# F in 64x64 tiles with its blocks ordered by the copies, and the masks of the first two groups back on VectorE

## The chip, the cores and the metric

The kernel runs on one core of a Trainium2 chip. The metric is the device time of one execution in microseconds; of the kernel before there are three: 876.13, 878.44 and 879.28 us, median 878.44. The profile is that of one execution whose span was 874.4 us. All data is 32-bit floating point at the inputs, except the two weight matrices of the feed forward, which the kernel converts from 64-bit on the chip.

The engines are called by their names or by the profile's short forms: TensorE (PE for matmuls, PEld for the loads of its weights), VectorE (DVE), ScalarE (ACT), GpSimd (POOL) and SyncE (SP, which here only issues transfers). PSUM is the memory that TensorE writes into.

## The reference

Two blocks follow each other: a recurrent attention with a state per batch and head, and a feed forward with a hard swish.

```python
batch, n_heads, seq, head_dim = (4, 8, 768, 40)
for t in range(S):
    y[:, :, t] = np.einsum('bhd,bhde->bhe', rt, state)
    Sa = np.einsum('bhde,bhe->bhd', state, at)
    state_decay = state * wt[:, :, None, :] - np.einsum('bhd,bhe->bhde', Sa, bt)
    state = state_decay + np.einsum('bhd,bhe->bhde', vt, kt)
# ... bridge: (B,H,S,D) -> (B*S, H*D) = (3072, 320)
h = x @ w_in                       # 320 -> 2048
relu6 = np.clip(h + 3.0, 0.0, 6.0)
g = h * relu6 / 6.0
return (g @ w_out)                 # 2048 -> 320
```

The kernel does not step through the 768 times one by one. It takes blocks of 64 times, and within a block it solves a triangular system: with the decays divided out, the products of all a with all earlier b in a block form a strictly triangular 64x64 matrix F per head, and the inverse of (1 - F) gives all `Sa` of the block at once. Products of k with a (called E), of v with r (C) and of u with r (H) are wanted for earlier times only, so these 64x64 scores are masked to a strict triangle.

## The kernel before

There are 24 units: 12 blocks of time by two pairs of batches; the two batches of a pair lie in the two halves of the partitions. Four units are a group; F of a group is kept for 4 x 8 = 32 heads, and its inverse is made on VectorE by substitution over 32 columns of the diagonal 32x32 blocks (`invert`, 60 small products and sums with waits between), after which TensorE adds the off-diagonal block (`third_block`). So F's 64x64 matrix of a head is used in two pieces: its two diagonal 32x32 blocks, which the inversion reads at columns 0 to 31 of F's tile, and the lower off-diagonal block, which `third_block` reads at columns 32 to 63 of the lower 32 rows.

The kernel has three phases. In the first, the four units of the first group are prepared by twos, the first inversion runs on VectorE, and the weights are converted by VectorE and ScalarE in small steps between. In the second, the four units of the first group take their scan steps in staggered chains, while the weights are finished and the second group is prepared. In the third, the stages of four units at a time and the feed forward of finished units share TensorE to the end. All engines take their instructions in the order in which the program emits them.

F of a unit, in tiles of 32 columns of at; each 32x64 result lands in its own quarter of the partitions, and for the lower rows (c = 1) the two 32-column halves of bt are read in reverse order, so that the diagonal block always lands at columns 0 to 31:

```python
        def f_stage():

            f = ps_pair(NPR, BL)
            for pr in range(NPR):
                for c in range(2):
                    for q in range(2):
                        for s in range(2):
                            x = q * BL + c * L
                            y = o["bt"][half(s, D), pr, half(q)].rearrange("p (c t) -> p c t", c=2)
                            if c:
                                y = y[:, ::-1, :]
                            z = (q ^ s) * BL + c * L
                            nc.tensor.matmul(out=f[s][z:z + L, pr, :],
                                             lhsT=o["at"][half(s, D), pr, x:x + L], rhs=y,
                                             start=True, stop=True, tile_position=(s * SLOT, z))
            yield PE
            for s in range(2):
                x = n * H + 4 * s
                nc.scalar.activation(out=F[:, x:x + 4, :], in_=f[s], func=AF.Copy, scale=-1.0)
```

The masks. In the first two groups (`early`) ScalarE copies the scores out of PSUM and GpSimd sets the unwanted triangle to zero; later VectorE copies only the wanted elements into a tile whose other elements stay zero:

```python
    def masked(o, early):

        turn[0] += 1
        x = score[turn[0] % len(score)]
        if early:
            for i in range(2):
                nc.scalar.activation(out=x[:, 4 * i:4 * i + 4, :], in_=o[i], func=AF.Copy)
            for q in range(2):
                nc.gpsimd.affine_select(
                    out=x[half(q)], in_=x[half(q)], pattern=[[0, H], [1, BL]],
                    compare_op=ALU.is_gt, fill=0.0, base=0, channel_multiplier=-1)
            return x
        for i in range(2):
            nc.vector.copy_predicated(out=x[:, 4 * i:4 * i + 4, :], mask=mask4, data=o[i])
        return x
# ...
            o["E"] = masked(x, i < 2 * NU)      # e_stage, NU = 4
# ...
            m["K"] = masked(x, i < NU)          # s_C
# ...
            m["B"] = masked(x, i < NU)          # s_H
```

The first stage of a step, with the fetch of the next unit's r (four transfers of 40 KB) on ScalarE's queue for units 1 to 3:

```python
        def s_RT():
            x = turn_pairs(o["RN"])
            yield PE
            m["RT"] = turned("RT")
            nc.scalar.activation(out=m["RT"][:], in_=x[:], func=AF.Copy)
            fetch("R", i + 1, nc.scalar if i < NU - 1 else nc.sync)
            scale = tmp.tile([P, 2, NPR], F32, name="scale", bufs=2)
            nc.gpsimd.tensor_tensor(out=scale[:], in0=last_dec[p][:], in1=dec[:, 0], op=ALU.mult)
            nc.gpsimd.tensor_copy(last_dec[p][:], dec[:, 1])
            nc.vector.tensor_tensor(out=st[:, :, :, 0:D], in0=st[:, :, :, 0:D],
                                    in1=_ap(scale[:], 0, [[NPR, 2], [1, NPR], [0, D]]), op=ALU.mult)
```

The conversion of a weight piece takes 5 steps; a step is a turn of this generator, and there are 40 pieces:

```python
                nc.vector.tensor_scalar(x, hi, 20, 0x7FF, ALU.logical_shift_right,
                                        ALU.bitwise_and)
                nc.scalar.activation(out=x, in_=x, func=AF.Relu, bias=low[:], scale=2.0 ** 23)
                yield
# ... (m likewise, then two scalar_tensor_tensor on VectorE)
                nc.vector.tensor_tensor(out=dst, in0=mf, in1=xf, op=ALU.mult)
                converted[0] += 1
                load()
                yield
```

The second phase, with the weight steps that go beside the stages:

```python
    for t in range(LAST + OWN):
        for i in range(NU):
            if 0 <= t - APART * i < OWN and t - APART * i != 11:
                if t - APART * i < 2:
                    block(i, t - APART * i)
                run(chains[i], weight=3 if t else 12)
        # ... the second group's loads and preparation
        elif t >= OWN + 1:
            pieces(1)                           # feed forward of finished units
```

Of the kernel before, what the change touches and what calls it, by code (L numbers as in the profile page):

```python
# [11 lines left out]
ALU = mybir.AluOpType  # L12
AF = mybir.ActivationFunctionType
# [3 lines left out]
P = 128  # L17
BL = 64
HB = BL // 2
L = 32  # L20
# [9 lines left out]
def kernel(  # L30
# [42 lines left out]
    nc = tc.nc  # L73
    B, H, T, D = r.shape
    NG = T // (2 * BL)
    NPR = H // 2
    NP = B // 2
    NU = 2 * NP
# [29 lines left out]
    def ps_pair(*dims):  # L108

        n = 1  # L110
        for d in dims:
            n *= d
        if shared[0] is None or shared[1] + n > 512:
            shared[:] = [ps_any([P, 512]) for _ in range(2)], 0
        at = shared[1]
        shared[1] += n
        views, step = [], n
        for d in dims:
            step //= d
            views.append([step, d])  # L120
        return [_ap(t[:], at, views) for t in shared[0]]
# [6 lines left out]
        out=ident[:], in_=ones, pattern=[[1, P]],  # L128
        compare_op=ALU.is_equal, fill=0.0, base=0, channel_multiplier=-1,
# [3 lines left out]
        out=ones[:, 0:BL], in_=ones[:, 0:BL], pattern=[[1, BL]],  # L133
# [185 lines left out]
    PE, DONE = 1, 2  # L319
# [4 lines left out]
    def fetch(name, i, engine=None):  # L324

        if i is None or i >= NK:
            return
        x, crossed = {"W": (w, 0), "A": (a, 0), "B": (b, 0), "K": (k, 0), "R": (r, 1),
                      "V": (v, 1)}[name]
        if name == "V":  # L330
            t = values[i % AHEAD]
        else:
            t = (others if i < 2 * NU and i % 2 and name != "R" else inputs)[name]
        g, p = names[i]
        engine = engine or nc.sync
# [30 lines left out]
    def half(i, n=SLOT):  # L366
        return slice(SLOT * i, SLOT * i + n)
# [10 lines left out]
                                     rhs=rhs[half(i, D), n, half(q)], start=True, stop=True)  # L378
        return o

    def masked(o, early):

        turn[0] += 1
        x = score[turn[0] % len(score)]
        if early:
            for i in range(2):
                nc.scalar.activation(out=x[:, 4 * i:4 * i + 4, :], in_=o[i], func=AF.Copy)
            for q in range(2):
                nc.gpsimd.affine_select(  # L389
                    out=x[half(q)], in_=x[half(q)], pattern=[[0, H], [1, BL]],  # L390
                    compare_op=ALU.is_gt, fill=0.0, base=0, channel_multiplier=-1)
            return x
        for i in range(2):
            nc.vector.copy_predicated(out=x[:, 4 * i:4 * i + 4, :], mask=mask4, data=o[i])  # L394
        return x


    def prepare(i, F):
# [45 lines left out]
            bt = o["bt"] = turned("bt")  # L444
            nc.vector.tensor_tensor(out=bt[:], in0=x[:], in1=o["rg"][:], op=ALU.mult)

        def f_stage():

            f = ps_pair(NPR, BL)
            for pr in range(NPR):  # L450
# [12 lines that stand above are left out]
            for s in range(2):  # L463
                x = n * H + 4 * s
                nc.scalar.activation(out=F[:, x:x + 4, :], in_=f[s], func=AF.Copy, scale=-1.0)

        def factor_stage():

# [28 lines left out]
        def e_stage():  # L497
            x = scores(o["kt"], o["at"])
            yield PE
            o["E"] = masked(x, i < 2 * NU)  # L500

        def ev_stage():

# [9 lines left out]
            for q in range(2):  # L513
# [1 line left out]
                    nc.scalar.activation(out=EV[half(q ^ s), s], in_=ev[q][half(q ^ s)], func=AF.Copy)  # L515
            o["EV"] = EV

        return {"W": w_stage, "gam": gam_stage, "A": a_stage, "B": b_stage, "F": f_stage,
                "factor": factor_stage, "K": k_stage, "E": e_stage, "EV": ev_stage}

    def in_turn(stages, order):
# [81 lines left out]
    def step(i):  # L603
# [6 lines left out]
        def s_RT():  # L610
            x = turn_pairs(o["RN"])
            yield PE
            m["RT"] = turned("RT")
            nc.scalar.activation(out=m["RT"][:], in_=x[:], func=AF.Copy)  # L614
            fetch("R", i + 1, nc.scalar if i < NU - 1 else nc.sync)
            scale = tmp.tile([P, 2, NPR], F32, name="scale", bufs=2)
            nc.gpsimd.tensor_tensor(out=scale[:], in0=last_dec[p][:], in1=dec[:, 0], op=ALU.mult)
            nc.gpsimd.tensor_copy(last_dec[p][:], dec[:, 1])
            nc.vector.tensor_tensor(out=st[:, :, :, 0:D], in0=st[:, :, :, 0:D],
                                    in1=_ap(scale[:], 0, [[NPR, 2], [1, NPR], [0, D]]), op=ALU.mult)  # L620
# [49 lines left out]
        def s_C():  # L670
            x = scores(m["VT"], m["RT"])
            yield PE
            m["K"] = masked(x, i < NU)

        def s_UT():

# [50 lines left out]
        def s_H():  # L727
            x = scores(m["UT"], m["RT"], swap=True)
            yield PE
            m["B"] = masked(x, i < NU)  # L730

        def s_y():
            y = ps_pair(NPR, BL)
# [154 lines left out]
    def run(stage, steps=0, weight=0, mixed=0):  # L888

        for at in stage:  # L890
            if at == DONE:
                return
            aside(steps, mixed)
            for _ in range(weight):
                next(weights, None)
# [64 lines left out]
    for t in range(LAST + OWN):  # L960
        for i in range(NU):
            if 0 <= t - APART * i < OWN and t - APART * i != 11:
                if t - APART * i < 2:
                    block(i, t - APART * i)
                run(chains[i], weight=3 if t else 12)
        if t == LAST + 2:
            seconds()
            for name in "WA":
                fetch(name, NU + 1)
            third.clear()  # L970
            second_group = by_twos(NU, 3, 0, 1.25)
# [98 lines left out]
    m = 0  # L1070
# [59 lines left out]
```

## Time and profile before

| engine | busy us | share of the span |
|---|---|---|
| TensorE, matmuls | 787.2 | 90% |
| TensorE, weight loads | 670.8 | 77% |
| VectorE | 529.8 | 61% |
| ScalarE | 297.2 | 34% |
| GpSimd | 177.1 | 20% |

A busy time is the union of an engine's instructions, so matmuls that overlap in different tiles of the array are not counted twice. In the groups, one row stands for all instructions of a line and form: `L459 PE MATMUL any<-bt,at 40*32 40x64` are matmuls with 40 rows and 32 columns of weights on 64 moving columns, from tiles bt and at into a PSUM tile called any. The trace has two matmul records for each 32-bit matmul. After the bar come the busy time and the mean of one in ns, then the idle time of the engine just before these instructions, and what ended it. In a timeline each row is a run of equal instructions: start, time, engine, line, count, and in brackets the idle time before it with its releaser. The line numbers are those of the kernel before; L389 and L387 are the selections and copies of the early masks, L394 the predicated copies, L459 and L465 the matmuls and copies of F.

The costliest matmuls are those of the feed forward: L839 with 231.9 us, L815 with 195.3 and L820 with 55.8. The longest idle time that the chain of waits names at the end is 7.59 us after the last matmul.

### The profile page before, as it was taken

How to read it: one execution, taken by the hardware profiler on the slowest of the kernel's cores; microseconds unless marked ns; L12 is line 12 of the kernel's file. 1: busy time of each engine (PE TensorE's matmuls, PEld its weight loads, DVE VectorE, ACT ScalarE, POOL GpSimd, SP SyncE). 2: the span in 40 equal slices, each digit the busy share in tenths (PEclk: the TensorE clock that was granted, in tenths of full speed). 3: DMA queues.
4: the chain of work that ended last, by engine and by line, in shares of the span. 5: the costliest groups of instructions: out<-in, count | busy, mean ns of one | idle time of the engine just before them, and what ended most of it. 6: DMA issues, size and time to landing. Idle time of an engine off the chain costs nothing.

```text
span 874.4 us, 36298 instructions
## 1 busy us (share of the span) xinstructions
PE 787.2 (90%) x16128; PEld 670.8 (77%) x16128; DVE 529.8 (61%) x1109; ACT 297.2 (34%) x726; POOL 177.1 (20%) x327
## 2 busy tenths in 40 slices
PE   4710987888999999999999999999999999999998
PEld 4510865777888788887888888888888888888886
DVE  7899777677855669834579543787545774221211
ACT  1433754333334322442322433223433224232211
POOL 4441122243112230320220221211212102000000
PEclk9755559999999999999999999999999999999999
DMA  6543443242033331322321222121232101100000
GB/s 132 88 108 92 123 116 85 48 75 45 14 52 61 57 59 26 60 37 42 59 40 36 56 49 49 39 50 34 45 62 42 24 21 27 24 21 12 19 18 15
DMA packets 175979, 45.08 MB, mean 52 GB/s; under 512 B 157904, under 2 KB 173264, under 8 KB 175824
## 3 DMA queue, kind: packets, MB, share of 16 engines
q1 hardware_dynamic: 171504, 42.12, 24.3%
q8 instruction: 127, 2.08, 1.0%
q10 hardware_dynamic: 4320, 0.66, 0.5%
q14 instruction: 28, 0.23, 0.1%
HBM read 34.08 MB, written 3.93 MB: 43 GB/s over the span
## 4 chain that ended last, share of the span: by engine, by line
PE 69%; DVE 5%; issue 3%; DMA 1%; ACT 1%; POOL 1%; SPq 0%; POOLq 0%; DVEq 0%; ACTq 0%
PE o L839 22%; PE h L815 18%; PE h L820 5%; PE any L358 5%; PE any L376 3%; PE any L717 2%; PE any L740 2%; PE any L459 2%; PE any L628 1%; PE any L593 1%; PE any L662 1%; PE any L581 1%; DVE x L558 1%; DVE prod L552 1%; PE any L699 1%
## 5 line engine op out<-in xcount | busy, mean ns | idle before, releaser
L839 PE MATMUL o<-wout,gt 128*128 128x320 f32 x768 | 231.9, 447 | 1.1 <-issue 1.1
L815 PE MATMUL h<-xt,win 128*128 128x128 f32 x1536 | 195.3, 280 | 0.4 <-DVE gt L826 0.4
L815 PEld LDWEIGHTS h<-xt,win 128*128 128x128 f32 x1536 | 184.0, 193 | 10.4 <-DVE gt L826 0.9
L839 PEld LDWEIGHTS o<-wout,gt 128*128 128x128 f32 x768 | 140.1, 191 | 55.7 <-issue 2.2
L826 DVE SCALAR_TENSOR_TENSOR gt<-gt,h 128x512 f32<-128x512 f32 x96 | 61.4, 681 | 110.3 <-ACT gt L825 110.3
L825 ACT ACTIVATE gt<-h,three 128x512 f32<-128x512 f32 x96 | 60.8, 684 | 157.5 <-PE h L820 157.5
L750 POOL TENSOR_TENSOR yg<-ys,gam 128x512 f32<-128x512 f32 x24 | 41.1, 1715 | 193.9 <-DVE ys L747 130.8
L552 DVE TENSOR_TENSOR prod<-x 128x30 f32<-128x30 f32 (+9 forms) x180 | 63.7, 354 | 12.9 <-POOL x L543 8.2
L482 POOL TENSOR_TENSOR KBt<-K,rgt 128x320 f32<-128x320 f32 x24 | 24.5, 1022 | 221.5 <-ACT rgt L474 207.8
L558 DVE TENSOR_TENSOR x<-x,prod 128x30 f32<-128x30 f32 (+9 forms) x180 | 63.6, 353 | 4.4
L820 PE MATMUL h<-xt,win 64*128 64x128 f32 x768 | 55.8, 285 | 0.0
L820 PEld LDWEIGHTS h<-xt,win 64*128 64x128 f32 x768 | 46.6, 187 | 5.3 <-issue 0.2
L421 DVE RECIPROCAL gam<-prods 128x256 f32<-128x256 f32 x24 | 41.4, 1739 | 13.4 <-POOL yg L750 13.1
L747 DVE TENSOR_TENSOR ys<-any,ys 128x256 f32<-128x256 f32 x48 | 18.1, 419 | 49.8 <-PE any L509 29.7
L410 DVE TENSOR_TENSOR_SCAN prods<-wm,start 128x528 f32<-128x528 f32 x24 | 30.1, 1253 | 22.7 <-ACT wm L407 21.1
L724 DVE TENSOR_TENSOR state<-any,state 128x160 f32<-128x160 f32 x48 | 13.2, 316 | 49.1 <-PE any L376 49.1
L436 DVE RECIPROCAL rgam<-prods 128x256 f32<-128x256 f32 x24 | 41.7, 1737 | 0.0
L394 DVE COPY_PREDICATED score<-mask,any 128x256 f32<-128x256 int32 x112 | 41.3, 433 | 0.0
L581 PE MATMUL any<-tb,F 32*32 32x32 f32 x768 | 16.0, 199 | 24.9 <-DVE tb L561 24.8
L267 ACT ACTIVATE parts<-parts,low 128x256 uint32<-128x256 uint32 x40 | 20.3, 508 | 49.8 <-DVE parts L265 45.6
L740 PE MATMUL any<-score,KBt 64*64 64x64 f32 x1536 | 31.1, 227 | 6.2 <-POOL score L389 6.2
L614 ACT ACTIVATE RT<-any 128x512 f32<-128x512 f32 x24 | 14.3, 596 | 65.2 <-PE any L358 65.1
(138 smaller groups left out, 1205.8 us busy)
## 6 DMA issues: line engine op xcount, KB each, us to landing
raw<-in_moe_w_out_dram SPq DMA_DIRECT2D x20, 256.0 KB
B<-in_b_dram SPq DMA_DIRECT2D x48, 80.0 KB
K<-in_k_dram SPq DMA_DIRECT2D x48, 80.0 KB
V<-in_v_dram SPq DMA_DIRECT2D x96, 40.0 KB
out_dram<-ob SPq DMA_DIRECT2D x48, 80.0 KB
R<-in_r_dram SPq DMA_DIRECT2D x84, 40.0 KB
W<-in_w_dram SPq DMA_DIRECT2D x40, 80.0 KB
A<-in_a_dram SPq DMA_DIRECT2D x40, 80.0 KB
```

What stands on the lines that cost most here:

```text
L358: nc.tensor.transpose(out=o[:, n, :], in_=x[:, 2 * n:2 * n + 2, :].rearrange("p s e -> p (s e)"), identity=ident[:])
L394: nc.vector.copy_predicated(out=x[:, 4 * i:4 * i + 4, :], mask=mask4, data=o[i])
L421: nc.vector.reciprocal(gv[:, :, 0:HB], o["prods"][:, :, 0, 1:HB + 1][:, :, ::-1])
L436: nc.vector.reciprocal(rv[:, :, HB:BL], o["prods"][:, :, 1, 1:HB + 1])
L552: nc.vector.tensor_tensor(out=pv, in0=_ap(x[:], (i + 1) * L + i, [[L, n], [0, i]]), in1=_ap(x[:], i * L, [[0, n], [1, i]]), op=ALU.mult,)
L558: nc.vector.tensor_tensor(out=rest, in0=rest, in1=pv, op=ALU.add)
L740: nc.tensor.matmul(out=y[q][half(s), pr, :], lhsT=o[name][half(q), h * D:h * D + SLOT], rhs=m[name][half(q), 4 * rs + 2 * s + j, :], start ...
L815: nc.tensor.matmul(out=hp[c][:, i, :], lhsT=win[:, t, j * P:(j + 1) * P], rhs=xt[:, t, :], start=(t == 0 and i == 0), stop=False)
L820: nc.tensor.matmul(out=hp[c][:, i, :], lhsT=win2[half(c), (j0 + i) * P:(j0 + i + 1) * P], rhs=xt[half(c), 2, :], start=False, stop=(i == N ...
L825: nc.scalar.activation(out=gt[:], in_=hp[c][:], func=AF.Relu, bias=three[:], scale=1.0)
L826: nc.vector.scalar_tensor_tensor(out=gt[:], in0=gt[:], scalar=6.0, in1=hp[c][:], op0=ALU.min, op1=ALU.mult)
L839: nc.tensor.matmul(out=op[:], lhsT=gts[c][:, n, :], rhs=wout[:, c * HJ + r * NQ + n, :], start=((split or r == 0) and c == 0 and n == 0), ...
```

## The change

F is made in 64x64 tiles from the ninth unit on: a matmul takes 64 columns of at in place of 32, so there are half as many, and the reversal of the halves for the lower rows is done by the copies out of PSUM, which take each quarter of the partitions by itself. The upper 32 rows need only their first 32 columns. It is for TensorE, which is given fewer instructions for the same products. In place of this the kernel before has three other arrangements, which go: the early masks on ScalarE and GpSimd, which were to take work from VectorE, the r of units 1 to 3 on ScalarE's queue, and 12 weight steps in the first turn of the second phase.

```diff
-    def masked(o, early):
-
+    def masked(o):
         turn[0] += 1
         x = score[turn[0] % len(score)]
-        if early:
-            for i in range(2):
-                nc.scalar.activation(out=x[:, 4 * i:4 * i + 4, :], in_=o[i], func=AF.Copy)
-            for q in range(2):
-                nc.gpsimd.affine_select(
-                    out=x[half(q)], in_=x[half(q)], pattern=[[0, H], [1, BL]],
-                    compare_op=ALU.is_gt, fill=0.0, base=0, channel_multiplier=-1)
-            return x
         for i in range(2):
             nc.vector.copy_predicated(out=x[:, 4 * i:4 * i + 4, :], mask=mask4, data=o[i])
         return x
# ... f_stage is renamed f_by_32, and beside it stands
+        def f_by_64():
+
+            f = ps_pair(NPR, BL)
+            for pr in range(NPR):
+                for q in range(2):
+                    for s in range(2):
+                        nc.tensor.matmul(out=f[s][half(q ^ s), pr, :],
+                                         lhsT=o["at"][half(s, D), pr, half(q)],
+                                         rhs=o["bt"][half(s, D), pr, half(q)],
+                                         start=True, stop=True)
+            yield PE
+            for s in range(2):
+                x = n * H + 4 * s
+                for z in range(0, P, BL):
+                    nc.scalar.activation(out=F[z:z + L, x:x + 4, 0:L], in_=f[s][z:z + L, :, 0:L],
+                                         func=AF.Copy, scale=-1.0)
+                    y = f[s][z + L:z + BL].rearrange("p r (c t) -> p r c t", c=2)
+                    nc.scalar.activation(
+                        out=F[z + L:z + BL, x:x + 4, :].rearrange("p h (c t) -> p h c t", c=2),
+                        in_=y[:, :, ::-1, :], func=AF.Copy, scale=-1.0)
# ...
-            o["E"] = masked(x, i < 2 * NU)
+            o["E"] = masked(x)
# ... (s_C and s_H likewise)
-        return {"W": w_stage, "gam": gam_stage, "A": a_stage, "B": b_stage, "F": f_stage,
+        return {"W": w_stage, "gam": gam_stage, "A": a_stage, "B": b_stage, "F": f_by_32 if i < 2 * NU else f_by_64,
# ... in s_RT
-            fetch("R", i + 1, nc.scalar if i < NU - 1 else nc.sync)
+            fetch("R", i + 1)
# ... in the second phase
-                run(chains[i], weight=3 if t else 12)
+                run(chains[i], weight=3)
```

More of the change, by code (lines that the diff above doesn't have):

```diff
@@ L445, in b_stage, with f_by_32 @@
             nc.vector.tensor_tensor(out=bt[:], in0=x[:], in1=o["rg"][:], op=ALU.mult)
-        def f_stage():
+        def f_by_32():
             f = ps_pair(NPR, BL)
@@ L672, in s_C @@
             yield PE
-            m["K"] = masked(x, i < NU)
+            m["K"] = masked(x)
         def s_UT():
@@ L729, in s_H @@
             yield PE
-            m["B"] = masked(x, i < NU)
+            m["B"] = masked(x)
         def s_y():
```

## The prediction

> **What bounds the kernel now.** I read the page's table of slices first, because a mean hides stages with different limits.
>
> ```profile
> PE   4710987888999999999999999999999999999998
> DVE  7899777677855669834579543787545774221211
> PEclk9755559999999999999999999999999999999999
> ```
>
> A slice is 874.4 / 40 = 21.9 us. From slice 9 on (about 180 us) TensorE is busy 90% or more to the end: what is saved there counts only if it is TensorE time. Before that there are two other stages: slices 2 and 3, in which TensorE is nearly idle and VectorE full (the first inversion and the conversion of the weights), and slices 4 to 8, in which TensorE works at half clock or waits (the first four scan steps). The table by stretches gives the sizes (columns: stretch, its length, busy us and count of PE, PEld, DVE, ACT, POOL, then clock, DMA share, GB/s):
>
> ```profile
> 60.00:80.00 20.00, 0.00 (x0) 0.00 (x0) 20.00 (x75) 6.42 (x15) 0.00 (x0) 0.50 0.32 92
> ...
> 140.00:160.00 20.00, 15.57 (x334) 11.61 (x335) 10.29 (x29) 7.52 (x20) 4.48 (x8) 0.83 0.28 64
> ...
> 600.00:700.00 100.00, 100.00 (x2328) 86.66 (x2328) 57.34 (x109) 35.91 (x86) 22.68 (x39) 1.00 0.24 44
> ```
>
> Then the groups by form, for the durations of what is removed and added:
>
> ```profile
> L394 DVE COPY_PREDICATED score<-mask,any 128x256 f32<-128x256 int32 x112 | 41.3, 433 | 0.0
> L515 ACT ACTIVATE EV<-any 64x160 f32<-64x160 f32 x92 | 25.0, 295 | 26.6 <-PE any L509 14.8 <-DVE ys L747 11.3
> L389 POOL TENSOR_SCALAR_AFFINE_SELECT score<-score 64x512 f32<-64x512 f32 x32 | 22.7, 708 | 58.4 <-ACT score L387 57.1
> L459 PE MATMUL any<-bt,at 40*32 40x64 f32 x1440 | 20.2, 224 | 1.6 <-issue 1.2 <-DVE kt L495 0.2
> L376 PE MATMUL any<-at,kt 40*64 40x64 f32 x752 | 16.9, 221 | 1.3 <-ACT rgt L474 1.2
> L465 ACT ACTIVATE F<-any 128x256 f32<-128x256 f32 x45 | 14.8, 389 | 20.2 <-PE any L459 20.2
> ```
>
> and last the waits and the timeline of the step stage. The waits of 85 to 180 us have, among others:
>
> ```profile
> PEld any L740 <- POOL score L389: 7.2, 6, 4.2
> PE any L740 <- POOL score L389: 6.2, 5, 4.1
> ```
>
> and TensorE's timeline there shows the longest of them with what followed:
>
> ```profile
> 146.99 0.69 PE L740 MATMUL any<-score,KBt 64*64 64x64 f32 x32
> 151.80 0.47 PE L740 MATMUL any<-score,KBt 64*64 64x64 f32 x2 [4.11 <-POOL score L389]
> ...
> 154.46 2.40 PE L839 MATMUL o<-wout,gt 128*128 128x320 f32 x4
> ```
>
> The reader is to see two things: TensorE stood for 4.11 us for a mask of GpSimd, and after it four L839 matmuls took 2.40 us, where four take 1.34 us at other places (157.41). The wait cost its own length and a spell of half clock.
>
> **What the Trainium skill says.** "TensorE: Matmul & The Clock Gate", section "What's actually happening": the clock is halved after about 3.4 us without work and comes back after about 3.4 us of work. The trace agrees in kind: granted clock 0.50 from 152 to 155 us, 1.00 again from 158. It agrees less for the small matmuls: TensorE was busy 11.6 of the 12 us from 89 to 101 and stayed at 0.50; the clock came back only about 129 us, just after the first dense L815 matmuls (127.83). "SBUF — State Buffer", section "Who interferes with whom": a VectorE instruction with two inputs in SBUF excludes a GpSimd instruction that reads SBUF. The trace agrees: during the selections at 118.36 (1.57 us for two) the weight steps L278 and L280 took 0.87 us each, against 0.42 elsewhere. "TensorEngine Tiling (Array Packing)", section "PSUM Bottleneck": tiling speeds TensorE, not the copies out of PSUM. That is the risk of the first part of this change, from the other side: fewer matmuls, more copies.
>
> **Part 1, F in 64x64 tiles (16 units).** The compiled order of TensorE is the same in both kernels but for this: per unit 32 matmuls of 40x32 tiles become 16 of 40x64 (the trace counts two records for each). By starts in the timeline a lone F of one unit takes 0.79 us (182.10 to the next matmul at 182.89). The E scores are the very shape that F gets, and take 0.63 us alone (204.61 to 205.24) or 1.09 us for two units (186.95 to 188.04). So 0.16 to 0.24 us a unit, say 0.19, times 16 = 3.0 us of TensorE, in the stage where TensorE is the end. Against it, ScalarE copies: two of 128x256, back to back 0.67 us, become eight, four of 256 elements and four of 128. Back to back one of 256 takes 0.33, and one of 160 takes 1.11 / 4 = 0.28 (L515), so one of 128 about 0.25: 4 x (0.33 + 0.25) = 2.3 us, 1.6 us more a unit, 26 us in all. ScalarE is busy 36 of 100 us there, so it has the room; what may hurt is a copy that comes late for a bank or for the activation of the feed forward. At 406.53 the copies of F ran for 0.67 us and the next ScalarE instruction began at 408.98: 2.3 us just fits. I give back 0.5 us in all. Part 1: -2.5 us.
>
> **Part 2, the masks (16 of them: 8 of E, 4 of C, 4 of H).** Removed: 32 ScalarE copies (382 ns) and 32 GpSimd selections (708 ns), in series 0.65 + about 1.5 us and two hand-overs, some 2.4 us from scores to mask. Added: 32 predicated copies on VectorE, two in 0.76 us.
> First group (20 to 85 us), where VectorE is the bound: the first four copies (1.4 us) stand ahead of the reciprocals, but B's transposes come earlier too, whose waits (0.68 and 0.22 us before L445) then go: +0.5. The second four add 1.5 us, and VectorE gets back what the selections cost it: at 53.0 to 56.6 us four instructions took 0.69, 0.75, 0.79 and 0.87 in place of about 0.3, 0.3, 0.35 and 0.42, that is 1.7 us. Net about 0.
> Steps (85 to 175 us): the waits that end at a mask, or at ScalarE and GpSimd work queued behind one, are 0.39, 0.77, 1.47, 0.91, 0.47 and 4.11 us, together 8.1. VectorE has idle time here (10.29 of 20 busy in the row above), but the masks stand in its queue between weight steps: I take half of the small ones (2.0) and all but 1 us of the large (3.1), and 1.5 us of the half clock behind it: -6.6 us.
> Second group's E: waits of 2.3, 0.42 and 0.42 us at 206 to 211 us and again a half-clock spell (at 212 us), now with an inversion on VectorE between them: -2.5 us.
>
> **Part 3, r of units 1 to 3 from the SyncE queue, and 3 weight steps in place of 12 in the first turn.** The twelve issues held ScalarE's queue for 2.5, 3.1 and 5.0 us (89.0, 100.7 and 118.7), with copies between them; TensorE waited once behind that, 0.84 us for ys. Gone: -1 us. They now stand in SyncE's queue, which is continuously taken from 88 to 112 us by weights, at some 0.65 us each, 12 x 0.65 = 7.8 us. VectorE waited for raw weights there 4.2 us in all; later weights can make that more: +2 us. Nine weight steps fewer at the head (about 9 x 0.4 = 3.6 us of VectorE) free it for the first step, whose TensorE work waits for R's DMA (3.25 us) and the inversion anyway: 0. The two pieces of weights end later, at 152 to 160 us, where VectorE was idle for 6.18 us: 0.
>
> **Sum.** -2.5 + 0 - 6.6 - 2.5 - 1 + 2 = -10.6 us. What starts the stage of full TensorE earlier moves the end by as much, as long as the inputs of the second group keep pace: TensorE waited 2.67 us for K at 174.58, behind SyncE's queue, which is itself started by the results of the steps and so moves along. I hold back a little for that: -9.5 us, 878.4 - 9.5 = 868.9, so 869 us.
>
> **Rivals.**
> A: the masks were put on ScalarE and GpSimd because VectorE is full early, and taking them back costs what it gained. For: VectorE 20.00 of 20 us from 60 to 80, and 16 masks x 0.76 = 12 us of new work. If all of E's first group (3 us) and half of the steps' (3 us) lie on the path and no wait goes, 878 - 2.5 + 6 = 882. Against: the selections' price on VectorE itself, and the listed waits.
> B: the r fetches and weights in one queue become the bound of the steps: xt moves, R and raw weights in series from 136 to 149 us already made VectorE wait 2.64 us for raw weights. If that grows by 5 us it eats half of the gain: 874.
> C: the longer burst of F's copies delays activations or banks in the full stage, 0.5 us a unit: +8 us, 877. Against: ScalarE's idle gaps, most of them ended by TensorE (157.5 us before L825).
> D: with fewer waits the clock comes back sooner in the steps; TensorE at half clock from 85 to 128 us holds some 37 us of work. A return 10 us earlier would give another 4: 865. Against: it seems to follow the dense matmuls, which stay where they are.
>
> **Range and chances.** A to D span 865 to 882; the gain in the steps is the least certain term, since a wait removed there often uncovers another on the same in-order queue. I take 859 to 879 for 8 in 10. Two per cent is 17.6 us: faster than 860.9 needs all of my gains and D (0.1), slower than 896 needs A twice over (0.02).
>
> **What would show it.** Step by step: F's records as 40*64 with about 0.6 us a unit, and no wait of TensorE that ends at L825 or at F's copies; no TensorE wait for a mask above 1 us at 130 to 152 us and no clock below 1.00 there; the first L581 at 82.5 within 1 us; the first dense matmul at about 125; the second K transposes some 6 us earlier than 177.39; VectorE's waits for raw weights at 4 to 7 us. The prediction is wrong if the first L581 comes over 2 us late (A), if raw weights are waited for over 8 us (B), or if the stretch of full TensorE from the second group to the end isn't 2 to 6 us shorter (C).

## Result, and the profile after

| kernel | median us (lowest to highest) | ratio to before (95% interval) |
|---|---|---|
| before | 878.15 (876.13 to 879.28) | |
| after | 864.7 (862.65 to 866.41) | 0.9848 (0.9816 to 0.988) |

The change takes 13.4 us off, 1.5%; 869 us had been predicted. (The table has one execution of the kernel before more than the three named above.) The profiled spans, 874.4 and 860.9 us, differ by 13.5 us, so the two traces can be compared stage by stage. I compare the starts of the same instructions; how much earlier the kernel after is at one of them is its lead.

| start of | before | after | lead | gained since the row above |
|---|---|---|---|---|
| first product of the first inversion (L581, in the kernel after L593) | 82.49 | 81.20 | 1.29 | 1.29 |
| first dense matmul of the feed forward (L815, L827) | 127.83 | 121.94 | 5.89 | 4.60 |
| W transposes of the second group | 159.31 | 152.04 | 7.27 | 1.38 |
| first state transposes of the second group | 242.22 | 234.54 | 7.68 | 0.41 |
| the same of the ninth unit | 366.00 | 359.28 | 6.72 | -0.96 |
| the same of the 16th unit | 581.64 | 569.70 | 11.94 | 5.22 |
| the same of the 20th unit | 704.73 | 691.26 | 13.47 | 1.53 |

From the 20th unit on the lead stays the same to the end. (The 7.59 us that the chain of waits names there in the kernel before do not follow the last matmul, as said above: TensorE's last L839 matmuls run beside them, from 861.61 to 870.12 us.) I call what lies behind the first state transposes of the second group the full stage. So 7.7 us come from the stages before TensorE is full, where the prediction had -6.6 - 2.5 + 1 = -8.1, and 5.8 from the full stage, where it had -2.5. The page's slices after:

```profile
PE   4710988798999999999999999999999999999998
DVE  7999677878845579834589553697446774221211
PEclk8755668998999999999999999999999999999999
```

Counted from 0, the clock digits 4 and 5 (about 86 to 129 us) are 6 and 6 in place of 5 and 5, so the half clock is now broken up there; digit 6 is 8 in place of 9, and so is digit 9. The table by stretches (columns as in the prediction):

```profile
140.00:160.00 20.00, 15.76 (x339) 12.34 (x338) 15.10 (x31) 6.44 (x19) 3.57 (x9) 0.91 0.42 86
...
600.00:700.00 100.00, 100.00 (x2104) 86.40 (x2100) 60.12 (x120) 39.71 (x103) 19.00 (x34) 1.00 0.22 42
```

VectorE still fills 60 to 80 us (20.00 of 20 us there). From 140 to 160 us VectorE works 15.1 us where it was 10.3, and TensorE is no busier. From 600 to 700 us TensorE starts about 2100 matmul records where it started 2328, with ScalarE 4 us busier. The groups by form:

```profile
L472 ACT ACTIVATE F<-any 32x128 f32<-32x128 f32 x64 | 16.9, 264 | 13.2 <-PE any L464 12.4
L464 PE MATMUL any<-bt,at 40*64 40x64 f32 x512 | 10.9, 219 | 0.5 <-issue 0.5
L475 ACT ACTIVATE F<-any 32x256 f32<-32x256 f32 x64 | 24.0, 375 | 0.7
```

A unit of F is 32 records and the eight copies take 4 x (264 + 375) = 2.56 us of ScalarE, where two took 0.78. A copy of 32x256 takes 375 ns and one of 128x256 took 389: four times as many partitions make hardly a difference, the elements per partition do.

The waits from 85 to 180 us (columns: what waits, for what, us in all, times, longest):

```profile
DVE parts L265 <- DMA raw<-in_moe_w_out_dram: 5.4, 2, 3.5
DVE parts L265 <- DMA raw<-in_moe_w_in_dram: 3.1, 2, 2.4
PE any L752 <- DVE score L385: 2.3, 1, 2.3
```

The 4.11 us wait for GpSimd's mask is gone, but TensorE now waits 2.33 us for VectorE's (both times for the mask of H, which the second half of these L740 or L752 matmuls reads), and VectorE waits 5.4 + 3.1 = 8.5 us for raw weights, against 4.2 before. The timelines show that these are one thing. TensorE's:

```profile
142.42 0.69 PE L752 MATMUL any<-score,KBt 64*64 64x64 f32 x32
145.44 1.25 PE L752 MATMUL any<-score,KBt 64*64 64x64 f32 x32 [2.33 <-DVE score L385]
147.44 2.15 PE L851 MATMUL o<-wout,gt 128*128 128x320 f32 x4
```

VectorE's:

```profile
140.26 0.43 DVE L285 TENSOR_TENSOR wout<-parts 128x256 f32<-128x256 f32 x1
144.21 0.29 DVE L265 TENSOR_SCALAR parts<-raw 128x256 uint32<-128x256 uint32 x1 [3.52 <-DMA raw<-in_moe_w_out_dram]
144.41 0.28 DVE L270 TENSOR_SCALAR parts<-raw 128x256 uint32<-128x256 uint32 x1
144.62 0.42 DVE L278 SCALAR_TENSOR_TENSOR parts<-raw,parts 128x256 f32<-128x256 uint32 x1
144.95 0.76 DVE L385 COPY_PREDICATED score<-mask,any 128x256 f32<-128x256 int32 x2
```

and the issues of SyncE's queue (second column: how long the issues hold the queue):

```profile
133.76 0.39 SPq L249 DMA_DIRECT2D raw<-in_moe_w_out_dram  x1
134.27 3.74 SPq L341 DMA_DIRECT2D R<-in_r_dram  x4
138.06 3.03 SPq L781 DMA_DIRECT2D xt<-yg  x4
141.19 1.55 SPq L249 DMA_DIRECT2D raw<-in_moe_w_out_dram  x3
```

The next raw weights are issued at 141.19, behind four R and four xt transfers that hold the queue for 6.8 us; VectorE stands at L265 for them until 144.21; the mask is three instructions behind it in the same queue; TensorE waits for the mask, and the four L851 after it run at half clock again (2.15 us for what takes 1.34).

### The profile page after: what moved, and what is told of

Read it like the earlier page. It is cut to its first block, busy times and chain, and to the rows that moved or that the text cites. A ratio compares the mean times of both kernels' runs of the same rounds, so it can differ in the third digit from the quotient of the medians.

```text
span 860.9 us, 35329 instructions
## 1 busy us (share of the span) xinstructions
PE 777.6 (90%) x15616; PEld 663.4 (77%) x15616; DVE 535.8 (62%) x1141; ACT 317.5 (37%) x790; POOL 152.7 (18%) x295
## 4 chain that ended last, share of the span: by engine, by line
PE 68%; DVE 6%; issue 3%; POOL 1%; ACT 1%; DMA 0%; SPq 0%; POOLq 0%; DVEq 0%
PE o L851 22%; PE h L827 18%; PE h L832 5%; PE any L358 5%; PE any L376 3%; PE any L729 2%; PE any L752 2%; DVE x L570 1%; DVE prod L564 1%; PE any L674 1%; PE any L640 1%; PE any L593 1%; PE any L605 1%; PE any L711 1%; PE any L695 1%
## 5 line engine op out<-in xcount | busy, mean ns | idle before, releaser
L851 PE MATMUL o<-wout,gt 128*128 128x320 f32 x768 | 231.7, 447 | 0.0
L827 PE MATMUL h<-xt,win 128*128 128x128 f32 x1536 | 194.7, 279 | 0.8 <-DVE gt L838 0.7
L827 PEld LDWEIGHTS h<-xt,win 128*128 128x128 f32 x1536 | 183.2, 192 | 10.7 <-DVE gt L838 1.6
L851 PEld LDWEIGHTS o<-wout,gt 128*128 128x128 f32 x768 | 140.0, 191 | 54.4 <-issue 1.6
L494 POOL TENSOR_TENSOR KBt<-K,rgt 128x320 f32<-128x320 f32 x24 | 22.7, 945 | 215.2 <-ACT rgt L486 201.5
L385 DVE COPY_PREDICATED score<-mask,any 128x256 f32<-128x256 int32 x143 | 52.9, 432 | 0.0
L412 DVE RECIPROCAL gam<-prods 128x256 f32<-128x256 f32 x24 | 41.4, 1738 | 13.4 <-POOL yg L762 13.2
L267 ACT ACTIVATE parts<-parts,low 128x256 uint32<-128x256 uint32 x40 | 20.3, 508 | 56.4 <-DVE parts L265 56.1
L593 PE MATMUL any<-tb,F 32*32 32x32 f32 x768 | 15.1, 195 | 26.2 <-DVE tb L573 26.2
L593 PEld LDWEIGHTS any<-tb,F 32*32 32x32 f32 x768 | 13.8, 111 | 28.9 <-issue 27.4
```

The source lines that it names most:

```text
L412: nc.vector.reciprocal(gv[:, :, 0:HB], o["prods"][:, :, 0, 1:HB + 1][:, :, ::-1])
L827: nc.tensor.matmul(out=hp[c][:, i, :], lhsT=win[:, t, j * P:(j + 1) * P], rhs=xt[:, t, :], start=(t == 0 and i == 0), stop=False)
L851: nc.tensor.matmul(out=op[:], lhsT=gts[c][:, n, :], rhs=wout[:, c * HJ + r * NQ + n, :], start=((split or r == 0) and c == 0 and n == 0), ...
```

## Experiments

Each ratio is to executions of the kernel before on the same chip (medians there 876.98, 877.25 and 878.33 us), and a difference in us is that ratio applied to that median; a difference of two medians can be another by up to 1.6 us. A lead is from one profile each; before the full stage such leads vary from kernel to kernel by a few us (the kernel after without F's new tiles does the same as the kernel after up to the ninth unit, and is 3.4 us ahead where that is 7.7; its TensorE waits 4.11 us for S at 130.9 us, which the kernel after does not), so times in that part rest on the waits and on the ratios.

The questions: is the gain the masks', as the prediction had it, or F's; in F, do the tiles bring it and do the copies cost something; what do the masks cost on VectorE; and do late weights (SyncE's queue) or the masks themselves make the new wait.

### The four parts alone

**F alone.** In before: `f_by_32` and `f_by_64` as in the change, and nothing else.

```diff
-        return {..., "F": f_stage,
+        return {..., "F": f_by_32 if i < 2 * NU else f_by_64,
```

> The kernel before with F in 64x64 tiles from the ninth unit on and nothing else. Theory 1 (F's gain is TensorE time in the full stage): 878.2 - 16 x 0.2 = 875, and down to 873 if the short stalls after F (1.2 to 1.5 us, three of them in the kernel before) go as well. Rival (the lead gained after the second group comes from elsewhere, and F's longer copies eat its TensorE time): 877 to 879.

Measured: 873.35 us, 0.9953 (0.9935 to 0.9971), so -4.1 us. The lead is 0.06 at the second group and 5.56 at the end.

**The masks alone.** In before:

```diff
-            o["E"] = masked(x, i < 2 * NU)
+            o["E"] = masked(x, False)
-            m["K"] = masked(x, i < NU)
+            m["K"] = masked(x, False)
-            m["B"] = masked(x, i < NU)
+            m["B"] = masked(x, False)
```

> The kernel before with all early masks on VectorE and nothing else. Theory 1 (the masks are the early gain, since they end waits of TensorE and free VectorE's port): 868 to 872. Rival (r's fetches and the weight steps at the head are the early gain, and the masks only load a full VectorE): 877 to 882.

Measured: 871.6 us, 0.994 (0.9918 to 0.9962), so -5.3 us. The 4.11 us wait for a mask became one of 3.7 us for VectorE's mask.

**r on SyncE's queue alone.** In before:

```diff
-            fetch("R", i + 1, nc.scalar if i < NU - 1 else nc.sync)
+            fetch("R", i + 1)
```

> The kernel before with the fetches of r of units 1 to 3 on SyncE's queue and nothing else. Theory 1: between -1 and +2 us, so 877 to 880. Rival: the twelve issues held ScalarE for 10 us, and TensorE's waits behind ScalarE go with them: 872 to 875.

Measured: 878.08 us, 1.0019 (1.0008 to 1.0031), so +1.6 us.

**Three weight steps alone.** In before:

```diff
-                run(chains[i], weight=3 if t else 12)
+                run(chains[i], weight=3)
```

> The kernel before with 3 weight steps in place of 12 in the first turn of the second phase and nothing else. Theory 1: no change, 877 to 879, since the first step waits for r's transfer and the inversion. Rival: the head of the first step is freed by 3.6 us of VectorE, 874 to 876.

Measured: 875.34 us, 0.9979 (0.9965 to 0.9994), so -1.8 us.

The four add up to -4.1 - 5.3 + 1.6 - 1.8 = -9.6 us; the whole gives -13.4. The intervals of the five leave about 4 us open, so these times don't show that the parts bring more together than apart. The next two take one part out of the whole.

### The whole without one part

**Without F's new tiles** (the edits of the masks, of r and of the weight steps together).

> The changed kernel with F as it was (32-column tiles, two copies): masks, r on SyncE and 3 weight steps together. The parts alone measured -5.4, +1.1 and -1.6 us at the medians, sum -5.9. If the parts only add up: 871. If they help each other (the masks' wait for late weights goes only when fewer weight steps stand ahead), the whole is 864.7 plus the 3.6 to 4.1 us of F: 868 to 869.

Measured: 870.2 us, 0.9928 (0.9908 to 0.9949), -6.3 us; the other three parts alone add to -5.5, so these three do little more than add up. What F brings in company is 5.5 us by the two medians (870.2 and 864.7, not taken side by side) and 7.1 by the two ratios, with some 3 us of uncertainty. In the full stage this kernel gains 0.9 us on before and the kernel after 5.8, so F brings 4.9 us there; alone it brings 5.5 there. By the traces F's gain is about the same alone and in company.

**With r on ScalarE's queue** (the edits of F, of the masks and of the weight steps).

> The changed kernel with r of units 1 to 3 on ScalarE's queue again. If r on SyncE costs here what it costs alone (1 to 2 us): 862.5 to 863.5, faster than both kernels. If the other parts turn it into a gain (ScalarE's queue is what TensorE waits for once the masks are gone): 866 to 869.

Measured: 864.62 us, 0.9872 (0.985 to 0.9894): not to be told from the kernel after by the medians; by the ratios it may be some 2 us slower, but the intervals overlap. The traces show two costs that for the most part cancel. With r on ScalarE's queue TensorE waits 0.95 and 1.31 us for ys, 0.76 for RT and 0.59 for VT between 94 and 122 us, and the first dense matmul starts at 126.00, where it starts at 121.94 after and at 122.24 to 122.67 in the three other kernels that have all masks on VectorE, r on SyncE's queue and 3 weight steps. ScalarE's timeline of this kernel:

```profile
101.27 2.23 ACTq L341 DMA_DIRECT2D R<-in_r_dram  x2
103.55 0.66 ACT L727 ACTIVATE ys<-any 128x256 f32<-128x256 f32 x2 [2.08 <-PE any L614]
```

The copy ys stands behind the issues of R. The bracket names TensorE, which is what the copy's semaphore came from; the queue had held it until 103.5 all the same. But in the same kernel the raw weights are waited for 2.9 + 2.6 = 5.5 us from 80 to 240 us, and no TensorE wait for a mask of the steps is left (E's mask, at about 200 us, is still waited for, 1.3 us): by the W transposes it is 6.0 us ahead, the kernel after 7.3.

### F taken apart

**The tiles without the ordering copies.** In before, the matmuls of `f_by_64` for units nine on, with the two copies as before. This leaves out the exchange of the halves of the lower rows.

```diff
# ... the matmuls of f_by_64, then
+            for s in range(2):
+                x = n * H + 4 * s
+                nc.scalar.activation(out=F[:, x:x + 4, :], in_=f[s], func=AF.Copy, scale=-1.0)
```

> The kernel before with the 64x64 matmuls of F from the ninth unit on but the two plain copies of before: it leaves out the reordering of the lower rows' halves, so the numbers of F are other ones, the work of all else is the same. Theory (TensorE's part is 3.2 us of matmuls and 1.5 to 2 us of short stalls that the shorter burst of instructions avoids; the copies give some back): 877.2 - 5 = 872, and the wait of L640's counterpart (the product of state and at) for a mask at about 330 us is 0.8 us as in the kernel before, not 2.3. Rival (only the matmuls count, the copies cost nothing): 874, as with the whole of F.

Measured: 868.75 us, 0.9892 (0.9872 to 0.9912), -9.5 us, more than the theory or its rival gave.

**The copies without the tiles.** In before, for units nine on:

```diff
# ... units one to eight keep the two copies
+                for z in range(0, P, BL):
+                    nc.scalar.activation(out=F[z:z + L, x:x + 4, 0:L], in_=f[s][z:z + L, :, 0:L],
+                                         func=AF.Copy, scale=-1.0)
+                    nc.scalar.activation(out=F[z + L:z + BL, x:x + 4, :], in_=f[s][z + L:z + BL],
+                                         func=AF.Copy, scale=-1.0)
```

> The kernel before with F in its 32-column tiles, and only the copies split in eight as in the changed kernel (no reordering needed). Theory (the longer copies hold up the inversion and through it a mask): +1.5 to +2 us, 879, with the wait for a mask at about 330 us grown from 0.8 to 2.3 us. Rival (ScalarE has the room): 877, the wait as before.

Measured: 880.89 us, 1.0033 (1.0019 to 1.0048), +2.9 us.

In the full stage the first gains 8.25 us and the second loses 3.07; the sum, 5.2, is what F alone gains there (5.5). By the ratios the two add to -6.6, F alone is at -4.1; the difference of 2.5 us lies within the three intervals, and I don't read it as anything.

Where the tiles gain: TensorE's timeline of the kernel before, around F in the full stage,

```profile
340.68 0.65 PE L699 MATMUL any<-RT,S 40*64 40x64 f32 x32
341.26 0.86 PE L459 MATMUL any<-bt,at 40*32 40x64 f32 x64
342.05 1.34 PE L839 MATMUL o<-wout,gt 128*128 128x320 f32 x4
```

and of the kernel after:

```profile
333.96 0.65 PE L711 MATMUL any<-RT,S 40*64 40x64 f32 x32
334.43 0.65 PE L464 MATMUL any<-bt,at 40*64 40x64 f32 x32
335.01 1.88 PE L851 MATMUL o<-wout,gt 128*128 128x320 f32 x6
```

From start to start, F takes 342.05 - 341.26 = 0.79 us before and 335.01 - 334.43 = 0.58 after. The group ahead of it, L699 (L711 after), becomes shorter by the same reading: 0.58 before, 0.47 after. F's two values are the medians of all 16 units, and the 0.58 and 0.47 those of the 13 units in which F comes behind L699 (L711); in the three others it comes behind the 128-column transposes L471 (L483), which take 0.53 us to F's start in both kernels. So the change from 64-column tiles to tiles of 32 has a price of 0.11 us of its own where small tiles stand ahead. Together 16 x 0.21 + 13 x 0.11 = 4.8 us. There is a second gain, of another kind. Before, TensorE stops inside or right behind F's matmuls:

```profile
403.55 0.81 PE L459 MATMUL any<-bt,at 40*32 40x64 f32 x59
405.57 0.31 PE L459 MATMUL any<-bt,at 40*32 40x64 f32 x5 [1.21 <-issue]
```

"issue" says that the engine waited for nothing that the profile shows. I count what F takes to the start of the next group above 0.79 us: 1.47 us here (the next group starts at 405.81), 1.21 and 0.28 at two later units, 3.0 together before; with the copies alone 1.27, 1.52, 0.5 and 0.33. All eight kernels with the 32-column tiles have the stop near 400 us, and most have one or two of the later ones. With the 64-column tiles there is one, above 0.58 us, of 0.76 (after) to 1.17 us, and in two kernels a smaller second one. That is 3.0 - 0.76 = 2.2 us more for the kernel after. What makes TensorE stop isn't shown by any run.

Where the copies cost: TensorE's timeline with the tiles alone,

```profile
330.31 0.94 PE L643 MATMUL any<-state,at 40*64 40x40 f32 x29 [0.76 <-DVE score L394]
```

and with the copies alone:

```profile
332.33 0.94 PE L635 MATMUL any<-state,at 40*64 40x40 f32 x29 [2.30 <-DVE score L394]
```

In both this is the wait for a mask beside the third group's inversion. The inversion on VectorE starts, with a transposition of F, from F's copies; with eight of them it starts later, and the mask stands behind its first instructions. VectorE's timeline before,

```profile
315.75 2.17 DVE L540 STREAM_TRANSPOSE fb<-F 128x1024 f32<-128x1024 f32 x1 [1.30 <-ACT F L465]
```

and after:

```profile
309.40 2.19 DVE L552 STREAM_TRANSPOSE fb<-F 128x1024 f32<-128x1024 f32 x1 [3.08 <-ACT F L475]
```

F's matmuls of that unit start at 314.09 and 305.96, so the transposition follows them by 1.66 us before and by 3.44 after, 1.8 us more. Before, the wait for the mask is 0.77 us, after it is 2.33. With one gap of 0.31 us for F's copy at 270.02 that is 1.9 us, nearly all at this one place, not at every unit: at the ninth unit the lead falls (6.72 in the first table).

So for the full stage of the kernel after: 4.8 + 2.2 - 1.9 = 5.1 of the 5.8 us measured. For the tiles alone it is 4.8 + 2.1 = 6.9 of 8.25; the rest isn't found.

**Half of the copies on VectorE in each group's last unit** (on the kernel after).

```diff
# ... in a helper that makes each copy
+                if s and n == NU - 1:
+                    nc.vector.tensor_scalar(out, src, -1.0, None, ALU.mult)
+                else:
+                    nc.scalar.activation(out=out, in_=src, func=AF.Copy, scale=-1.0)
```

> The changed kernel with half of F's copies on VectorE in the last unit of each group from the third on (four units), so that F is complete for the inversion about 1.1 us sooner. If F's copies cost the full stage through the inversion: the wait of 2.3 us for a mask at 324 us falls to about 1, and the time by 1 to 1.5 us: 863.4. If VectorE's four more copies shift that wait instead: 864.7 or above.

Measured: 863.67 us, 0.9851 (0.9826 to 0.9876): no difference in the time that can be told. The wait for the mask went from 2.33 to 1.75 us: the transposition now follows F's matmuls by 2.89 us in place of 3.44, since VectorE takes 1.46 us for its four copies and then does L511 (0.69 us) ahead of it. The full stage gains 6.2 us on before in place of 5.8. Both fit the account, but 0.6 us is below what these times resolve, and more of the wait is left than goes.

### The masks taken apart

**E's masks alone** (in before, only the edit of `o["E"]`).

> The kernel before with only the eight masks of E on VectorE. As predicted from the waits: first group about 0, second group -2.5, so 874.5. Rival (VectorE is full in the first phase and bears four more copies at each of two places): 877 to 880.

Measured: 877.7 us, 1.0007 (0.9986 to 1.0027): not to be told from before. TensorE's timeline at the second group's EV:

```profile
207.52 0.94 PE L509 MATMUL any<-V,score 64*64 64x40 f32 x32 [2.25 <-issue]
210.21 1.42 PE L509 MATMUL any<-V,score 64*64 64x40 f32 x32 [1.75 <-DVE score L394]
```

and VectorE's just before:

```profile
205.12 0.83 DVE L558 TENSOR_TENSOR x<-x,prod 128x58 f32<-128x58 f32 x1
205.98 0.81 DVE L552 TENSOR_TENSOR prod<-x 128x84 f32<-128x84 f32 x1
206.98 0.76 DVE L394 COPY_PREDICATED score<-mask,any 128x256 f32<-128x256 int32 x2
208.84 0.26 DVE L552 TENSOR_TENSOR prod<-x 128x108 f32<-128x108 f32 x1
```

The waits of 2.3, 0.42 and 0.42 us of before (one of the short ones was for the transfer of b, not for a mask) are 2.25 and 1.75 now. The first, which the bracket puts down to issue, ends at 207.52, while the mask's two copies of 206.98 run. The mask has no selection before it, but it stands between steps of the second group's inversion, and these take 0.8 us each here where the same operation takes 0.26 later with more elements. GpSimd multiplies KBt at that time; that this is what makes the steps longer was not tried by itself. In the first group the first inversion starts 1.1 us earlier, and that is lost again by the W transposes (-0.15), where TensorE waits 4.9 us for GpSimd's mask of H.

**The masks of the steps alone** (in before, the edits of `m["K"]` and `m["B"]`).

> The kernel before with only the eight masks of C and H on VectorE. As predicted from the waits: -6.6, so 871. Rival (the wait of 4.11 us is for weights that come late, and stays as a wait for VectorE): 874 to 877.

Measured: 872.64 us, 0.9958 (0.9941 to 0.9974), -3.7 us. Its waits from 80 to 240 us:

```profile
PE any L740 <- DVE score L394: 4.4, 1, 4.4
DVE parts L265 <- DMA raw<-in_moe_w_out_dram: 9.1, 3, 4.4
```

The same 4.4 us twice: the large wait stays at full length and only changes its releaser, from GpSimd to VectorE, and VectorE is held up by raw weights. It is the same pair in the kernels without F (3.1 and 4.9), with the masks alone (3.7 and 3.7) and after (2.33 and 3.52). The 4.11 us wait of the kernel before can be followed one engine further in the same way. Its ScalarE timeline:

```profile
149.60 0.51 ACT L267 ACTIVATE parts<-parts,low 128x256 uint32<-128x256 uint32 x1 [3.16 <-DVE parts L265]
150.01 0.40 ACT L272 ACTIVATE parts<-parts 128x256 f32<-128x256 f32 x1
150.32 0.64 ACT L387 ACTIVATE score<-any 128x256 f32<-128x256 f32 x2
```

and its VectorE timeline:

```profile
149.27 0.29 DVE L265 TENSOR_SCALAR parts<-raw 128x256 uint32<-128x256 uint32 x1 [2.64 <-DMA raw<-in_moe_w_out_dram]
```

The copies of the scores (L387) stood on ScalarE behind the weight step L267, which waited for VectorE's L265, which waited for raw weights. The selections began right after, at 151.03. The scores had been ready since the matmuls L376 at 144.57, which take 0.82 us. By this reading the wait put down to GpSimd was in large part the wait for raw weights already; in the kernel before itself this was not tried, the next experiment tries it in the kernel after.

### SyncE's queue

If the late weights come from the queue, taking other transfers off it must remove the mask's wait; if the masks are too slow for VectorE, it must not. On the kernel after, the moves of finished rows (xt<-yg) of the first four units go to GpSimd's queue:

```diff
-                nc.sync.dma_start(out=dst, in_=src)
+                (nc.gpsimd if i < NU else nc.sync).dma_start(out=dst, in_=src)
# ... the same for the other four moves of a unit
```

> The changed kernel with the transfers of the first four units' results (xt from yg, eight of each unit) on GpSimd's queue in place of SyncE's. If the remaining wait for a mask at 145 us is for weights that come late behind these transfers in SyncE's queue: the raw-weight waits of VectorE fall from 8.5 us to under 4, the wait of 2.3 us goes, and the time falls by 2 to 4 us, to 861 to 863. If the weights are late because their buffers come free late, or GpSimd issues slowly: no gain, 864 to 868.

Measured: 860.18 us (858.67 to 860.79), 0.9796 (0.9779 to 0.9812): 4.5 us below the kernel after, 18 below before. Its waits from 80 to 240 us for raw weights, and TensorE's timeline at the mask:

```profile
DVE parts L265 <- DMA raw<-in_moe_w_in_dram: 0.3, 1, 0.3
DVE parts L265 <- DMA raw<-in_moe_w_out_dram: 0.2, 1, 0.2
```

```profile
140.35 1.38 PE L752 MATMUL any<-score,KBt 64*64 64x64 f32 x64
141.55 0.63 PE L674 MATMUL any<-RR,tinv 64*64 64x40 f32 x32
142.11 1.34 PE L851 MATMUL o<-wout,gt 128*128 128x320 f32 x4
```

Raw weights are waited for 0.5 us in place of 8.5, the mask of H comes without a wait, L851 takes 1.34 us (full clock), and the W transposes start at 146.99 in place of 152.04. This decides between the two: in the kernel after, the mask waits because of the queue. With r of units 1 to 3 on ScalarE's queue that wait was gone as well (above). The kernel with the moves is the fastest kernel of the study.

## Why the prediction was right, and where its terms were not

The time fell in the range, 4 us below the value given. The sum for the stages before TensorE is full was near (8.1 against 7.7), but by luck in part: the errors of its terms cancelled, and the 7.7 are of one pair of profiles (the kernel without F's tiles leads by 3.4 us at the same place; by its time the three other parts bring 6.3 us, with an interval of 4.5 to 8.1). The term for F was too small.

**"Part 1: -2.5 us" was mis-sized**: -4.1 us alone (interval 2.5 to 5.7), and by the traces of the full stage about 5. The 3.0 us of TensorE (16 x 0.19) were measured between neighbours that also have 64-column tiles or from lone groups, and left out what follows from the neighbours: F itself gives 0.21 a unit, the hand-over into 32-column tiles another 0.11 at 13 of 16 units, together 4.8 us; and the stops at F's matmuls, seen in the trace of before as "1.2 <-issue" in the group of L459 and not counted, give about 2.2. The 0.5 us given back for the copies were 1.9.

**Rival C was true in kind and wrong in shape.** Not 0.5 us at each of 16 units: 1.6 us once, at a mask behind an inversion that starts late, and 0.31 once more, for F's copy. The tiles alone give -9.5 us and the copies alone +2.9.

**"First group: net about 0"** held nearly: the first L593 comes 1.3 us early, outside the 1 us that was given for it, and 0.9 to 1.5 us early in every kernel with E's masks on VectorE.

**Steps, "-6.6 us": measured -3.7 alone (interval 2.3 to 5.2).** The step that failed is "all but 1 us of the large" wait (3.1 us) and with it 1.5 us of half clock. It took the releaser that the profile names, GpSimd's mask, for the cause. The wait stayed, at 2.33 us after and 4.4 with these masks alone. The 2.64 us wait for raw weights that holds it up in the kernel before stands in the prediction under rival B, and was not put together with it.

**"Second group's E: -2.5 us": measured about 0** (+0.6, interval -1.2 to +2.4). The inversion on VectorE was named and then left out of the sum; the mask's place between its steps kept the wait.

**r, "-1 us" and "+2 us"**: both signs held, and both were too small. +1.6 us alone; in company the issues on ScalarE's queue hold TensorE up for 0.95 + 1.31 + 0.76 + 0.59 = 3.6 us, and putting them on SyncE's queue loses 2.8 us of the 4.1 so gained at the first dense matmul again by the W transposes, through late weights. Raw weights were waited for 8.5 us, above the 8 us that the prediction gave as the mark of **rival B**: B was right that this queue is what the steps wait for, and the growth from 4.2 to 8.5 us is near the 5 us it named; the time did not rise with it, since the first dense matmul comes 5.9 us earlier and the wait for the mask behind the weights is 2.33 us where it was 4.11. Alone, r on SyncE's queue leaves TensorE waiting for ScalarE, which still copies the masks' scores: 1.4 us for these copies and 1.2 for VT from 85 to 130 us. With all masks on VectorE these copies are gone from ScalarE.

**Weight steps, "0": measured -1.8 us**, with an interval of about -0.5 to -3.1. The one profile of that kernel has a lead of 0.2 us at the end and doesn't show where the gain is; this stays open.

**Rival D came partly true, and the reason given against it was wrong.** Half clock was to last until the dense matmuls. After, it ended without them. TensorE's timeline:

```profile
95.28 1.20 PE L593 MATMUL any<-tb,F 32*32 32x32 f32 x64
96.41 0.66 PE L358 MATMUL any<-ident,R 128*128 128x128 f32 x4
102.28 0.88 PE L729 MATMUL any<-U,KBt 64*64 64x40 f32 x23 [1.14 <-issue]
103.08 1.11 PE L358 MATMUL any<-ident,V 128*128 128x128 f32 x4
```

The same four transposes take 0.66 us at 96.41 (full clock) and 1.11 at 103.08 (half). The first dense matmul, expected at 125, starts at 121.94. But this is not what brings the 4.6 us of this stage. With the moves on GpSimd's queue half clock lasted to 109 us, and the first dense matmul came at 122.67, only 0.7 us later than after; without F's tiles it lasted to 110 and the matmul came at 122.45; with r on ScalarE's queue, at 126.00. The issues of r on ScalarE's queue are the larger part.

Of the other marks: the second K transposes came 7.6 us earlier (6 predicted); 0.58 us for F (0.6); the wait for a mask above 1 us and a clock below 1.00 at 130 to 152 us, which were to be absent, are there, and one wait of 0.31 us ends at F's copies, where none was to be.

## What to carry to other kernels

A wait that one engine ends may hide a second cause with nearly the same end: before counting it as a gain, look at what the new releaser has ahead of it in its own in-order queue, down to the queue that issues its transfers. Where a queue of one engine's issues gates a stage, moving a few transfers to the queue of an engine with less to do can be worth about as much as moving arithmetic between engines (here 4.5 us for the moves of four units, 5.3 for all the early masks). In a stage bound by TensorE, count small matmuls by starts from one group to the next, neighbours included, and look for stops called "issue" inside long runs of small tiles.

## What the runs showed of the hardware that was not expected

- Half clock can end under small matmuls alone. In the kernel after the granted clock is 0.50 up to 94 us, 0.76 from 94 to 95 and 1.00 from 95 on, after about 8 us without a stop from 86.39 on; it falls again within the stop of 1.14 us that ends at 102.28 (0.65 from 101 to 102, then 0.50). In the kernel with the moves on GpSimd's queue TensorE ran without a stop from 86.94 to 110 us, and full clock came only at 109, after about 22 us. The Trainium skill, "TensorE: Matmul & The Clock Gate", section "What's actually happening", gives about 3.4 us for both directions; these traces show longer for the release and shorter for the loss, under small tiles.
- A group of 64 records of 40x32 tiles costs 0.11 us at its start after a group of 40x64 tiles, besides its own 0.79 us, and at some of them TensorE stops for up to 1.67 us; the profile does not show why. Open.
- A ScalarE copy out of PSUM costs by its elements per partition: 264 ns for 128 on 32 partitions, 375 for 256 on 32 partitions, 389 for 256 on 128 partitions. Splitting F's two copies by partitions made 2.56 us out of 0.78.
- Not tried: the moves on GpSimd's queue together with half of F's copies on VectorE; and the selections' price on VectorE apart from their effect on the masks.
